# State products of a gated linear attention in three 32-column tiles per head

## The chip, the cores and the metric

The kernel runs on one core of a Trainium2 chip. The metric is the time of one execution on the device in microseconds; each figure is a median of several runs. The profile is one execution seen by the hardware profiler, with times counted from the start of its span.

## The reference

A linear attention with complex, data-dependent decay (4 sequences, 8 heads, 768 steps, head size 48) is followed by a two-layer network with an ELU between the layers, on all 3072 tokens:

```python
def _attn_ref(q, k, v, a_re, a_im):
    B, H, S, D = q.shape                          # 4, 8, 768, 48
    mag = np.sqrt(a_re * a_re + a_im * a_im)
    scale = np.minimum(mag, 0.999) / (mag + 1e-06)
    a_re_n, a_im_n = (a_re * scale, a_im * scale)
    for t in range(S):
        ar, ai = (a_re_n[:, :, t, :, None], a_im_n[:, :, t, :, None])
        new_re = ar * S_re - ai * S_im
        new_im = ar * S_im + ai * S_re
        kv = np.einsum('bhd,bhe->bhde', k[:, :, t], v[:, :, t])
        S_re, S_im = (new_re + kv, new_im)
        y[:, :, t] = np.einsum('bhd,bhde->bhe', q[:, :, t], S_re)

def _moe_ref(x, w_in, w_out):                     # x: 3072 x 384, d_ff 2048
    h = x @ w_in
    g = np.where(h > 0.0, h, np.exp(np.minimum(h, 0.0)) - 1.0)
    return g @ w_out
```

The state of a head is a complex 48 x 48 matrix. The kernel holds its real and imaginary parts one under the other, as 96 features by 48 values.

## The kernel before

The work is cut into 12 **units**, u = 0 to 11. A unit is two sequences (n = 0, 1) and 128 steps; `where(u)` gives them, and the units of a pair of sequences alternate with those of the other, so units 10 and 11 are the last 128 steps. A unit's 128 steps are two chunks (c = 0, 1) of L = 64 steps. Decays become cumulative sums of logarithms and angles (ScalarE, VectorE); keys and queries are multiplied by the decays and by cosine and sine (`gated`, L1003), which gives 96 features per head in `gates["k"]` and `gates["q"]`, one head beside the next; the key tile has 32 more columns of zeros at its end.

From these, in each unit:

- `state_products(u, n)` (L1089 to L1111): for each head and chunk, the product of keys and values over the chunk's 64 steps. The weights are 64 rows of `gates["k"]`, the streamed operand the chunk's 48 value columns of the head. The result goes to one PSUM tile `g` per chunk, 128 partitions by 8 heads by 48. In units 10 and 11 the last chunk's state isn't needed, so there is one chunk in place of two. From unit 1 on, a head and chunk take two matmuls of 64 columns each. 128 columns are read from the start of the head's 96, so the last 32 belong to the next head and their rows of the result are never used.
- the scores (in `small`, L1216; matmul at L1224): 32 matmuls of keys with queries, 96 rows, 64 columns, into the two PSUM banks that `outs` gives; `masked` (L1229) multiplies them by the causal mask.
- `state_sums` (L1113 to L1128): VectorE adds the old state to the product (L1124), GpSimd multiplies by the chunk's decay (L1126).
- values and carried state: `valued_pe` (L1237, matmul at L1145) and `carried_pe` (L1245, matmul at L1154); the latter reads the 96 feature rows of the state alone.
- `copied` and `seam` bring the result into the form in which the layers read it.

The two layers of a unit (`layer_of`, L1795) use fewer, combined products: `mult` (matmul at L1542), with sums, copies and the ELU between them (`kept` L1555, `joint` L1558, `low` L1563 and L1564, `whole_of` L1567), and `product` (L1404) with `folded` (L1382) ahead of it.

The **order** is written by hand: `plan` holds each step with a time in slots, the loop from L1837 on and `put` (L1710) fill it, `SHIFT` moves single steps, and what has the same time stays in the order in which it was put. Each engine issues its part in that order. For units 3 to 11 the stretch around the change is, on PE: `state_products(u, 0)`, the scores, `state_products(u, 1)`, then products of the layer before. In unit 4 some layer products stand between the scores and the second block; in units 10 and 11 both blocks stand ahead of the scores. The lines that place it:

```python
            put(r + 28.2, small, u)
            for n in range(NB):
                put(r + 28.2, state_sums, u, 0, (n,))
                put(r + 28.2, masked, u, n)
            put(r + 28.2, state_products, u, 1)
```

`PAIRED` is 2. Units 0 to 2 have orders of their own. The scores take the two banks of `outs`, which the layer of the unit before also uses (`opened_banks`, L1527).

Of the kernel before, what the change touches and what calls it, by code (L numbers as in the profile page):

```python
# [13 lines left out]
ALU = mybir.AluOpType  # L14
# [491 lines left out]
def kernel(  # L506
# [12 lines left out]
    nc = tc.nc  # L519
# [40 lines left out]
    F = 2 * D  # L560
# [5 lines left out]
    BL = 32  # L566
# [15 lines left out]
    def work(shape, tag="w"):  # L582
        return ps.tile(shape, FP32, tag=tag, bufs=3, name=tag)
# [4 lines left out]
    def where(u):  # L588
        return u % (B // NB) * NB, u // (B // NB) * C
# [122 lines left out]
    def new(tag, bufs=1, shape=None):  # L712
        return sb.tile(shape or [C, NB, H, D], FP32, tag=tag, bufs=bufs, name=tag)
# [306 lines left out]
    PAIRED = 2  # L1020
# [64 lines left out]
    def states(u, n):  # L1085
        state_products(u, n)
        state_sums(u, n)

    def state_products(u, n):  # L1089

        x = nat[u]
        b, s = where(u)
        x["S", n] = [state.get(b + n)]
        if s == S - C:
            last = C // L - 1
        else:
            last = C // L
        x["G", n] = gs = [
            work([C, H, D], "w" if u else "mlp")
            for c in range(last)  # L1100
        ]
        for h in range(H):
            for c, g in enumerate(gs):
                k = gates["k"][ts(c, L), ds((n * H + h) * F, C)]
                parts = [(g[ts(i, HP), h], k[:, ts(i, HP)]) for i in range(2)]
                if u == 0:
                    parts = [(g[:, h], k)]
                for to, of in parts:
                    nc.tensor.matmul(  # L1109
                        to, lhsT=of, rhs=vn[u % 2][ts(c, L), n, ts(h, D)], start=True, stop=True,  # L1110
                    )  # L1111

    def state_sums(u, n, chunks=range(C // L)):  # L1113
        x = nat[u]
        for c, g in list(enumerate(x["G", n])):
            if c not in chunks:
                continue
            old = x["S", n][-1]
            new_s = new("S", 8, [C, H, D])
            wide = x["T"][:, n, c].unsqueeze(2).to_broadcast([C, H, D])  # L1120
            if old is None:
                nc.vector.tensor_tensor(out=new_s, in0=g, in1=wide, op=ALU.mult)
            else:
                nc.vector.tensor_tensor(out=new_s, in0=g, in1=old, op=ALU.add)  # L1124
                eng = nc.vector if u < 2 else nc.gpsimd
                eng.tensor_tensor(out=new_s, in0=new_s, in1=wide, op=ALU.mult)  # L1126
            x["S", n].append(new_s)
        state[where(u)[0] + n] = x["S", n][-1]  # L1128

# [43 lines left out]
    def scored(u):  # L1173

        x = nat[u]
        t = outs()
        state_products(u, 0 if u > PAIRED else 1)
        for n in range(NB):
            for h in range(H):
                for c in range(C // L):  # L1180
                    nc.tensor.matmul(
                        t[n][ts(c, L), ts(h, L)], lhsT=keys_of(n, h, c),
                        rhs=queries_of(n, h, c), start=True, stop=True,
                    )
        if u > PAIRED:
            state_products(u, 1)
        for n in range(NB):
            state_sums(u, 0 if u > PAIRED else 1, [n])
            x["a", n] = new("a", 2, [C, H, L])
            nc.vector.tensor_tensor(  # L1190
                out=x["a", n], in0=t[n].rearrange("p (h t) -> p h t", h=H),
                in1=mask.unsqueeze(1).to_broadcast([C, H, L]), op=ALU.mult,
            )
        if u > PAIRED:
            state_sums(u, 1)
# [391 lines left out]
    def pronounced():  # L1587
# [13 lines left out]
        out=ident, in_=ident, pattern=[[-1, C]], base=0, channel_multiplier=1,  # L1601
# [20 lines left out]
    parts = [("in", m) for m in range(NF // 2)] + [("out", m) for m in range(NF // WF)]  # L1622
# [323 lines left out]
```

## Time and profile before

| what | value |
|---|---|
| time, median of 3 runs | 625.51 us (624.91 to 625.74) |
| span of the profiled execution | 622.1 us |
| PE matmuls busy | 604.0 us (97%), 6980 records |
| PE weight loads busy | 549.2 us (88%), 6980 records |
| VectorE (DVE) / ScalarE (ACT) / GpSimd (POOL) busy | 507.8 / 415.8 / 196.2 us |
| granted TensorE clock | 0.9 or more of full speed in all but one fortieth of the span |

A time is that of the whole execution, some 3.4 us above the span from the first to the last instruction that the profile shows. In the lists of instructions, a row of the timeline gives the start, the time that the merged instructions take, the engine, the line, the operation, the tiles (out<-in), the shape and the number of instructions; in brackets stands the engine's idle time before it and what ended it. "64*64" is rows by columns of the tensor engine's array that a matmul uses, "64x48" its rows by streamed columns. "issue" means that nothing that the profile shows was waited for. A row of the DMA view gives a queue's packets, their MB, and their time as a share of 16 engines over the stretch; of a stretch of 0.1 us, 100% is thus 1.6 us, and a packet counts where it starts.

### The profile page before, as it was taken

Reading aid. Unit: us, or ns where it says so; the run is one execution under the profiler, and the core shown is the slowest. Engines: PE = TensorE matmul, PEld = TensorE weight load, DVE = VectorE, ACT = ScalarE, POOL = GpSimd, SP = SyncE. Lnnn points to the kernel's source line nnn. Section 1 sums busy time; section 2 is a strip of 40 time slices with the busy share of each in tenths; the row PEclk is TensorE's granted clock in tenths of the full one; section 3 lists DMA queues with packets and bytes.
Section 4 is the critical chain, followed back from the end, with each engine's and each line's share of the span. In section 5 each row is a group of like instructions: output and inputs, shape, how many; then the busy total and the mean of one; then the engine's idle time right before and its main releaser. Section 6 shows DMA issues by size and latency. Waiting matters only on the chain. (4 is left out here: it accounts for less than half of the span.)

```text
span 622.1 us, 16987 instructions
## 1 busy us (share of the span) xinstructions
PE 604.0 (97%) x6980; PEld 549.2 (88%) x6980; DVE 507.8 (82%) x790; ACT 415.8 (67%) x681; POOL 196.2 (32%) x256
## 2 busy tenths in 40 slices
PE   8899999999999999999999999999999999999996
PEld 5778886576899999989999989998999999999996
DVE  6999999877688998988888888888788888884482
ACT  6985573776868667576777776776777777661350
POOL 2010000113123625623634534533544542522000
PEclk9899999999999999999999999999999999999999
DMA  9988669431623346355456354564574564252101
GB/s 173 181 154 144 129 174 199 111 78 44 103 42 66 62 88 141 71 121 129 96 118 140 82 120 107 117 120 97 121 122 100 136 109 116 56 95 65 54 1 32
DMA packets 192179, 65.54 MB, mean 105 GB/s; under 512 B 168116, under 2 KB 181596, under 8 KB 192092
## 3 DMA queue, kind: packets, MB, share of 16 engines
q1 hardware_dynamic: 187920, 62.72, 48.3%
q0 software_dynamic: 3520, 1.20, 1.7%
q8 instruction: 57, 0.93, 0.6%
q10 hardware_dynamic: 652, 0.44, 0.2%
q14 instruction: 30, 0.25, 0.1%
HBM read 48.91 MB, written 4.80 MB: 86 GB/s over the span
## 5 line engine op out<-in xcount | busy, mean ns | idle before, releaser
L1404 PE MATMUL mlp<-w_out,g 128*128 128x192 f32 x640 | 111.9, 328 | 0.0
L1404 PEld LDWEIGHTS mlp<-w_out,g 128*128 128x128 f32 x640 | 104.3, 190 | 3.3 <-DVE ee L1418 0.6
L1126 POOL TENSOR_TENSOR S<-S,T 128x384 f32<-128x384 f32 x36 | 38.1, 1059 | 143.3 <-DVE S L1124 84.6
L1382 DVE TENSOR_TENSOR g<-g 128x512 f32<-128x512 f32 x80 | 60.7, 774 | 6.3 <-PE mlp L1404 4.7
L1295 PE MATMUL mlp<-x,w_in 128*128 128x256 f32 x288 | 64.0, 380 | 0.2 <-DMA x<-y 0.2
L1295 PEld LDWEIGHTS mlp<-x,w_in 128*128 128x128 f32 x288 | 54.2, 190 | 8.9 <-ACT n L851 0.8
L1563 ACT ACTIVATE ee<-g 128x512 f32<-128x512 f32 x63 | 39.6, 628 | 30.1 <-DVE g L1558 27.6
L1542 PE MATMUL mlp<-x,w_in 128*128 128x128 f32 x424 | 56.6, 276 | 1.2 <-DVE o L1430 1.2
L1404 PE MATMUL mlp<-w,g 128*128 128x192 f32 x320 | 54.5, 329 | 0.0
L1275 POOL DMA_DIRECT2D x<-y x62 | 30.4, 498 | 71.6 <-ACT y L1171 39.1
L1542 PEld LDWEIGHTS mlp<-x,w_in 128*128 128x128 f32 x424 | 51.5, 192 | 1.5 <-DVE o L1430 1.4
L1404 PEld LDWEIGHTS mlp<-w,g 128*128 128x128 f32 x320 | 51.8, 190 | 0.6
L1567 DVE SCALAR_TENSOR_TENSOR g<-ee,g 128x512 f32<-128x512 f32 x63 | 44.2, 709 | 5.2 <-ACT ee L1564 5.2
L1564 ACT ACTIVATE ee<-ee 128x512 f32<-128x512 f32 x72 | 45.4, 631 | 2.3
L1555 ACT COPY g<-mlp 128x512 f32<-128x512 f32 x36 | 21.0, 586 | 25.7 <-PE mlp L1542 25.6
L1558 DVE TENSOR_TENSOR g<-g,mlp 128x512 f32<-128x512 f32 x45 | 30.4, 675 | 9.3 <-PE mlp L1542 8.1
L1542 PE MATMUL mlp<-x,g 128*128 128x128 f32 x224 | 30.0, 277 | 1.4 <-ACT g L1555 1.4
L1285 ACT ACT_TABLE_LOAD x24 | 30.8, 1283 | 0.5
L913 ACT ACTIVATE n<-w 64x384 f32<-64x384 f32 (+1 forms) x60 | 28.1, 486 | 3.8 <-PE w L898 3.0
L1262 ACT COPY x<-y 128x384 f32<-128x384 f32 x20 | 8.6, 482 | 31.4 <-PE y L1154 31.4
L1542 PEld LDWEIGHTS mlp<-x,g 128*128 128x128 f32 x224 | 27.7, 192 | 1.8 <-ACT g L1555 1.8
L1542 PE MATMUL y<-x,w_in 128*128 128x128 f32 x216 | 28.6, 275 | 0.5 <-ACT g L1555 0.5
(222 smaller groups left out, 1386.1 us busy)
## 6 DMA issues: line engine op xcount, KB each, us to landing
w<-in_moe_w_out_dram SPq DMA_DIRECT2D x8, 768.0 KB, 4.5
g<-in_moe_w_in_dram SPq DMA_DIRECT2D x24, 256.0 KB, 3.2
g<-in_moe_w_out_dram SPq DMA_DIRECT2D x24, 256.0 KB, 2.8
w<-in_moe_w_in_dram SPq DMA_DIRECT2D x16, 288.0 KB, 6.1
vn<-in_v_dram SPq DMA_DIRECT2D x24, 192.0 KB, 3.6
qt<-kt SPq DMA_DIRECT2D x72, 64.0 KB, 2.9
kt<-cs SPq DMA_DIRECT2D x72, 64.0 KB, 2.3
q<-in_q_dram SPq DMA_DIRECT2D x11, 384.0 KB, 4.5
```

Of the source, the lines that this page charges most:

```text
L913: nc.scalar.activation(out=flat(x[key][to, n : n + 1]), in_=t[of], func=AF.Exp, scale=sign)
L1126: eng.tensor_tensor(out=new_s, in0=new_s, in1=wide, op=ALU.mult)
L1275: eng.dma_start(out=x["x"][ds(j * HP + D, G), i], in_=x["y"][ds(j * HP + i * G, G)])
L1285: nc.scalar.preload_act_table_set(name)
L1295: nc.tensor.matmul(t[:, e], lhsT=w_in[:, i, ts(f + e, C)], rhs=x["x"][:, i], start=(i == 0), stop=(i == NI - 1),)
L1382: nc.vector.tensor_tensor(out=S_of(u, k, h), in0=a, in1=b, op=op)
L1404: nc.tensor.matmul(to, lhsT=a[:, m], rhs=b[:, m], start=(first and h == 0 and m == 0), stop=False, skip_group_check=True,)
L1542: nc.tensor.matmul(x["c" + c][:, ts(m, C)], lhsT=a[:, m], rhs=x["mix"][p], start=(p == BANKS[c][0] and m == 0), stop=False, skip_group_che ...
L1558: nc.vector.tensor_tensor(out=part(u, to), in0=part(u, a), in1=part(u, b), op=op)
L1563: nc.scalar.activation(out=e, in_=part(u, of), func=AF.Relu, scale=-1.0)
L1564: nc.scalar.activation(out=e, in_=e, func=AF.Exp, scale=-1.0)
L1567: nc.vector.scalar_tensor_tensor(out=part(u, to), in0=nat[u]["e", to], scalar=-1.0, in1=part(u, of), op0=ALU.add, op1=ALU.max,)
```

## The change

From the fourth unit on (u = 3 to 11), a head and chunk of `state_products` take three matmuls with 32 weight columns each, that write 32 partitions each, in place of two with 64. They cover the 96 features and nothing of the next head. `state_sums` then works on the 96 partitions that are written, in place of 128. The order of the steps stays.

```diff
@@ -1103,6 +1103,8 @@
             for c, g in enumerate(gs):
                 k = gates["k"][ts(c, L), ds((n * H + h) * F, C)]
                 parts = [(g[ts(i, HP), h], k[:, ts(i, HP)]) for i in range(2)]
+                if u > PAIRED:
+                    parts = [(g[ts(i, BL), h], k[:, ts(i, BL)]) for i in range(F // BL)]
                 if u == 0:
                     parts = [(g[:, h], k)]
                 for to, of in parts:
@@ -1118,12 +1120,16 @@
             old = x["S", n][-1]
             new_s = new("S", 8, [C, H, D])
             wide = x["T"][:, n, c].unsqueeze(2).to_broadcast([C, H, D])
+            to = new_s
+            if u > PAIRED:
+                to, g, wide = new_s[0:F], g[0:F], wide[0:F]
+                old = None if old is None else old[0:F]
             if old is None:
-                nc.vector.tensor_tensor(out=new_s, in0=g, in1=wide, op=ALU.mult)
+                nc.vector.tensor_tensor(out=to, in0=g, in1=wide, op=ALU.mult)
             else:
-                nc.vector.tensor_tensor(out=new_s, in0=g, in1=old, op=ALU.add)
+                nc.vector.tensor_tensor(out=to, in0=g, in1=old, op=ALU.add)
                 eng = nc.vector if u < 2 else nc.gpsimd
-                eng.tensor_tensor(out=new_s, in0=new_s, in1=wide, op=ALU.mult)
+                eng.tensor_tensor(out=to, in0=to, in1=wide, op=ALU.mult)
             x["S", n].append(new_s)
         state[where(u)[0] + n] = x["S", n][-1]
 
```

## Rows read from the trace of the kernel before

**Rows 1.** The page: busy time, the chain that ended last, the instruction queue (packets, MB).

```profile
PE 604.0 (97%) x6980; PEld 549.2 (88%) x6980; DVE 507.8 (82%) x790; ACT 415.8 (67%) x681; POOL 196.2 (32%) x256
...
PE mlp L1404 18%; PE mlp L1542 10%; PE y L1542 5%; PE y L1224 2%; PE y L1154 2%; PE w L1109 1%; PE y L1145 1%; PE w L846 1%; DVE g L1567 1%; DVE g L1558 1%; POOL kg L1014 1%; DMA g<-in_moe_w_in_dram 0%; DMA g<-in_moe_w_out_dram 0%; PE w L898 0%; ACT L1285 0%
```

**Rows 2.** Line L1109: xcount, then ns min/median/max of one, starts, forms.

```profile
L1109 PE MATMUL w<-vn,kg x1280: 199/218/253, 51.8 to 556.8; 64*64 64x48 f32 x183
```

**Rows 3.** Timeline of PE, the opening of unit 3.

```profile
179.34 1.15 PE L1109 MATMUL w<-vn,kg 64*64 64x48 f32 x64
180.42 2.09 PE L1224 MATMUL y<-qt,kt 96*64 96x64 f32 x64
182.43 1.15 PE L1109 MATMUL w<-vn,kg 64*64 64x48 f32 x64
183.51 0.76 PE L1404 MATMUL mlp<-w_out,g 128*128 128x192 f32 x3
```

**Rows 4.** Timeline of PE, both state blocks of unit 10.

```profile
509.34 2.07 PE L1109 MATMUL w<-vn,kg 64*64 64x48 f32 x64
```

**Rows 5.** Timeline of PE, two products with 48 weight columns (units 0 and 11).

```profile
14.80 0.88 PE L955 MATMUL w<-ident,n 128*48 128x2 f32 x16
...
565.56 1.99 PE L1154 MATMUL y<-qt,S 96*48 96x64 f32 x64
```

**Rows 6.** Timeline of PE and DVE, the opening of unit 7.

```profile
368.86 1.15 PE L1109 MATMUL w<-vn,kg 64*64 64x48 f32 x64
...
369.66 0.68 DVE L1558 TENSOR_TENSOR g<-g,mlp 128x512 f32<-128x512 f32 x1
...
370.00 2.44 PE L1224 MATMUL y<-qt,kt 96*64 96x64 f32 x64
...
372.38 0.56 PE L1109 MATMUL w<-vn,kg 64*64 64x48 f32 x24
...
373.47 0.80 PE L1109 MATMUL w<-vn,kg 64*64 64x48 f32 x40 [0.53 <-issue]
...
374.20 1.57 PE L1404 MATMUL mlp<-w_out,g 128*128 128x192 f32 x8
```

**Rows 7.** Timeline of PE, the opening of unit 8.

```profile
415.75 1.15 PE L1109 MATMUL w<-vn,kg 64*64 64x48 f32 x64
...
419.21 1.02 PE L1109 MATMUL w<-vn,kg 64*64 64x48 f32 x53
421.33 0.43 PE L1109 MATMUL w<-vn,kg 64*64 64x48 f32 x11 [1.10 <-issue]
421.69 1.57 PE L1404 MATMUL mlp<-w_out,g 128*128 128x192 f32 x8
```

**Rows 8.** Stretch between two stops: its length, then busy time (xcount) of each engine.

```profile
373.46:421.32 47.86, 46.73 (x633) 44.63 (x633) 39.35 (x64) 34.15 (x55) 22.22 (x25) 1.00 0.53 111
```

**Rows 9.** DMA queues from 180.3, 226.85, 278.3, 325.0, 370.75, 418.4, 466.3, over 0.1; then 373.46:421.32.

```profile
q8 instruction: 1, 0.02, 54.8%
...
q8 instruction: 1, 0.02, 69.2%
...
q8 instruction: 1, 0.02, 74.3%
...
q8 instruction: 1, 0.02, 70.9%
...
q1 hardware_dynamic: 106, 0.02, 99.0%
q8 instruction: 1, 0.02, 74.9%
...
q8 instruction: 1, 0.02, 83.3%
...
q8 instruction: 1, 0.02, 78.0%
...
q8 instruction: 5, 0.08, 0.8%
```

## The prediction

> **What bounds the kernel now.** I read the page first. TensorE's matmuls are busy for 97% of the span, no other engine for more than 82%, and the chain that ended last runs through PE lines, L1404 and L1542 ahead of all [rows 1]. So the kernel is bound by PE's stream: a microsecond more or less in its program order is a microsecond at the end, unless PE then meets a wait. The line of the edit has 1,280 matmul records at 64x64 [rows 2]; a float32 matmul leaves two matmul and two weight-load records, so a block of 32 matmuls (one sequence, two chunks) is 64 + 64 records.
>
> Next the PE timeline at the opening of a unit, which is where the change lies: a block of state products (S0), the scores, a second block (S1), then the layer's products [rows 3]. A block's 64 matmul records take 1.15 us, the last of them 0.22 us [rows 2, 3], so 63 steps take 0.93: 14.8 ns each, or 59 ns for the four tiles (two chunks, two column halves) that run side by side. Where the sequence has one chunk left, 64 records take 2.07 us [rows 4]: 29.4 ns each, again 59 ns per round, now of two tiles. So a tile's own turn sets the pace, and the other tiles run beside it.
>
> **What a 32-column tile costs.** No row has one. Bounds come from two neighbours. A record of 48 weight columns and 2 streamed ones comes every (0.88 - 0.18)/15 = 46 ns, so weights of 32 columns cost no more than that. A record of 48 weight columns and 64 streamed ones takes 56 ns per round of two ((1.99 - 0.22)/63 x 2), and 48 streamed columns in proportion 42 ns [rows 5]. The turn of a 64x32 tile with 48 streamed columns thus lies between 42 and 46 ns; I take 43, nearest to the streamed bound, since weights of 32 columns should load below 46. A head still needs two rounds (six tiles each, three where one chunk is left). A block of eight heads then takes 16 x 43 ns = 0.68 us in place of 0.93, provided that six tiles do run side by side; the other end is 14.8 ns per record whatever the tile, 96 x 14.8 = 1.42 us. I take 0.68, because the round's length did not change between two tiles and four.
>
> Where does this saving of 0.25 us a block land? In unit 3 on both blocks (0.5). In units 5 to 9 the scores, which begin at 370.00 in unit 7, get no further than their first matmul until DVE's L1558 frees their bank at 369.66 + 0.68 = 370.34, 1.48 us after S0 began [rows 6]. A shorter S0 only lengthens that wait, so S1 alone gains there, 0.25 each, and in unit 4 likewise. Units 10 and 11 run 32 rounds in one stretch: 32 x (59 - 43) = 0.5 each. Sum: -(0.5 + 0.25 + 5 x 0.25 + 2 x 0.5) = **-3.0 us**. DVE's and POOL's sums of states work on 96 partitions in place of 128; they have the same 384 elements in each, and I cost the difference at nothing, as PE does not wait for them here. No step, DMA or wait is moved.
>
> **What the added instructions cost.** In units 7 and 8, S1 stops in its middle, where no instruction waits for another engine: after 24 of 64 records, resuming at 373.47 [rows 6], and after 53, resuming at 421.33 [rows 7]. Between these two resumptions lie 1,266 PE records [rows 8] and five transfers of the instruction queue of 16 KB each [rows 9], so some 253 a transfer; with the dozen semaphore instructions 5 x 256 fits. Both stops, then, are the same edge of a block of 256 instructions that had not arrived. The transfer before the first stop starts at about 370.8 and takes 1.20 us (74.9% of 16 engines over 0.1 us), to 372.0; PE resumes 1.5 us later. At the second it is 418.45 + 1.33 = 419.8, and again 1.5 us later PE resumes [rows 6, 7, 9]. Counting 256 instructions back from the stops, PE had passed the edge before at 369.24 and 416.55. So passing an edge calls for the block after next, and from there to the resumption it took 4.2 and 4.8 us; PE, in dense code, got there sooner. Counting on from these edges, the same sum (start, length, 1.5 us) gives 2.8 us in unit 3 (edge 179.9), 3.5 in unit 4 (226.0), 3.3 in unit 5 (277.7), 2.9 in unit 6 (324.7) and 3.9 in unit 9 (465.2) [rows 9]. In unit 3 the data queue is idle; in unit 7 it is full beside the fetch [rows 9].
>
> Before, an opening has 3 x 128 = 384 PE instructions, and the second edge falls inside it only by luck. After, it has 192 + 128 + 192 = 512, two blocks, so **every opening of units 3 to 9 holds two edges 256 instructions apart**. Each unit also shifts the edges of the later ones by 128. Counted through the program, the first edge then lies 74, 35, 188, 118, 48, 234 and 164 instructions after S0's start in units 3 to 9. In time from S0's start, with S1 beginning at 3.5 us as in unit 7 [rows 6]: unit 5 passes its first edge at 188/192 x 0.68 = 0.67 us and reaches the second, 124 of 192 into S1, at 3.5 + 0.44 = 3.94.
>
> For the fetch I take the mean of the six loaded units, (3.5 + 3.3 + 2.9 + 4.2 + 4.8 + 3.9)/6 = 3.8 us, and 2.8 in unit 3; bounds 2.8 and 4.8. Unit 5: ready at 0.67 + 3.8 = 4.47, the 68 instructions left take 0.24, the change of tiles 0.15: 4.86, against 3.49 + 0.93 + 0.15 = 4.57 now, +0.29. Units 6 and 9 end at 4.86 too, against 4.54 now: +0.32 each. Unit 7: ready at 3.97, late in the scores, end 5.18 against 5.34 now (it loses its old stop), -0.16. Unit 8: edges at 2.10 and 4.06, ready at 5.90, end 6.13 against 5.94 now, +0.19. Unit 4: ready at 3.92 against 3.3 reached, +0.63, less 0.25: +0.38. Unit 3: ready at 3.06 against 2.88, so -0.5 shrinks to -0.31. Units 10 and 11 have one edge in their opening: -0.5 each. Sum: -0.31 + 0.38 + 0.29 + 0.32 - 0.16 + 0.19 + 0.32 - 1.0 = **+0.03 us**. The sum is against the span of 622.1 us; the median of the runs lies 3.4 above it, and I carry that over.
>
> The Trainium skill bears on this ("Runtime: NRT & Kernel Launch", section "Instruction fetch mechanics"): instructions come in 16 KiB blocks of 256, and a block's edge is said to be mostly hidden, since the next block is fetched while one executes. The block agrees with rows 9; that it is hidden does not, by the two stops.
>
> **Rivals.** *A, forecast: fetch takes back what the tiles give*, +0.03 us, 625.6. For it: the count of edges and six fetch lengths. Against: the lengths are not the new ones, as the edges are passed at other moments of the data traffic.
>
> *B, the blocks arrive in time.* New edges come earlier in the opening than the bulk of the data transfers in some units. With 2.8 us throughout: unit 3 -0.31, units 4, 5, 6 and 9 -0.25 each, unit 7 -1.0 and unit 8 -0.8 (mostly their old stops), units 10 and 11 -1.0: -4.1 us, 621.4. If blocks were always there, as the page of the skill has it, it would be -3.0 and the two stops' 2.0: -5.0 us, 620.5.
>
> *C, slower: the blocks come as late as in the two stops seen.* With their mean, 4.5 us, units 4 to 9 give +1.07, +0.99, +1.02, +0.54, +0.89, +1.02, and units 3, 10, 11 together -1.31: +4.2 us, 629.7. The place is S1 (the scores in units 4 and 7). Each 0.1 us of fetch is worth 0.6 us, so it decides from 4.0 us on. For it: these two are the only lengths that a resumption shows whole, and their edges are passed, as the new ones, within the first microsecond of an opening. Against: four other units are shorter.
>
> *D, six tiles don't overlap*, 14.8 ns per record: a block takes 1.42 us, some +1 us in each of units 3 to 9, -0.45 in units 10 and 11: about +6.1 us, 631.6. Against it: a round was 59 ns with two tiles and with four.
>
> That the change is without effect on the program is excluded: each head has three products in place of two.
>
> **How the numbers follow.** A 0.42, B 0.27, C 0.24, D 0.07. About 0.2% (1.25 us) is what a measurement of this kernel can tell from no change. A falls within it in most of its spread (0.36 of 0.42), the rest to both sides: faster 0.30, same 0.36, slower 0.34. The range leaves out the far half of B and nearly all of D: 622.0 to 629.8; A's own range, fetch 3.6 to 4.0 us, is 624.4 to 626.8.
>
> **What would show it.** Blocks of the state products of 96 records in about 0.9 us with the last one, not 1.6; in the timeline of units 4 to 9 a stop marked "issue" inside S1, or late in the scores in units 4 and 7, 1.5 us after an instruction transfer ends; units 10 and 11 half a microsecond shorter. Stops over 1 us in most units are C, none is B. The prediction is wrong in its steps if the stops sit elsewhere, or if the openings keep their length and the time moves in the layer's products.

## The result and the profile after

The kernel with the change takes 633.04 us (median of four runs, 631.25 to 634.07), against 625.3 us for the kernel before, measured beside it: a ratio of fast runs of 1.0131, 95% interval 1.011 to 1.0152 (the two medians alone give 1.012). It is slower by 7.7 us, outside the range of the prediction. The nearest number is that of rival D (631.6), but the profile below doesn't bear out D's mechanism; it shows that of C, with a larger loss. The profiled execution has a span of 632.3 us and a time of 634.06, which is 1.0 above the median.

Lines of the file move by six behind the change: the products of states are at L1111, the scores at L1230, the sums at L1130 (VectorE) and L1132 (GpSimd). First the page of the kernel after: busy time, TensorE's granted clock in 40 slices, and the instruction queue (packets, MB, share).

```profile
PE 606.2 (96%) x7492; PEld 549.7 (87%) x7492; DVE 505.9 (80%) x790; ACT 415.8 (66%) x681; POOL 207.2 (33%) x256
...
PEclk9899999999999999999999999998999999999999
...
q8 instruction: 61, 1.00, 0.7%
```

PE has 512 records more than in [rows 1]: 32 for each of the 14 blocks of units 3 to 9, and 32 for each of units 10 and 11. Its busy time grew by 2.2 us, while the span grew by 10.2. What was added is time in which PE stood still. The waits of PE by line (total us, times, longest us) name it:

```profile
PE w L1111 <- issue: 7.0, 4, 2.3
PE y L1230 <- issue: 2.4, 5, 1.7
```

"Issue" means that no semaphore was waited for. Before, only the two stops of [rows 6, 7] stood on the products' line, 1.6 us together. PE's timeline shows where the new ones lie. Units 4 (one row), 5, 6, 7, 8, 9 and 10 of the kernel after (start us, us, engine, line, operation, tiles, records, idle before):

```profile
228.49 0.68 PE L1230 MATMUL y<-qt,kt 96*64 96x64 f32 x14 [0.26 <-issue]
...
276.89 1.09 PE L1111 MATMUL w<-vn,kg 64*32 64x48 f32 x96
278.13 2.39 PE L1230 MATMUL y<-qt,kt 96*64 96x64 f32 x64 [0.15 <-issue]
280.44 0.79 PE L1111 MATMUL w<-vn,kg 64*32 64x48 f32 x62
283.13 0.47 PE L1111 MATMUL w<-vn,kg 64*32 64x48 f32 x34 [1.90 <-issue]
283.53 0.76 PE L1410 MATMUL mlp<-w_out,g 128*128 128x192 f32 x3
...
328.64 0.44 PE L1111 MATMUL w<-vn,kg 64*32 64x48 f32 x27
329.92 0.84 PE L1111 MATMUL w<-vn,kg 64*32 64x48 f32 x69 [0.84 <-issue]
...
373.47 1.09 PE L1111 MATMUL w<-vn,kg 64*32 64x48 f32 x96
374.76 2.15 PE L1230 MATMUL y<-qt,kt 96*64 96x64 f32 x56 [0.21 <-DMA g<-in_moe_w_in_dram]
378.63 0.45 PE L1230 MATMUL y<-qt,kt 96*64 96x64 f32 x8 [1.72 <-issue]
379.01 1.09 PE L1111 MATMUL w<-vn,kg 64*32 64x48 f32 x96
...
425.14 0.99 PE L1111 MATMUL w<-vn,kg 64*32 64x48 f32 x85
428.43 0.30 PE L1111 MATMUL w<-vn,kg 64*32 64x48 f32 x11 [2.30 <-issue]
...
471.90 1.09 PE L1111 MATMUL w<-vn,kg 64*32 64x48 f32 x96
473.14 2.39 PE L1230 MATMUL y<-qt,kt 96*64 96x64 f32 x64
475.46 0.69 PE L1111 MATMUL w<-vn,kg 64*32 64x48 f32 x50
478.12 0.64 PE L1111 MATMUL w<-vn,kg 64*32 64x48 f32 x46 [1.97 <-issue]
...
520.24 1.56 PE L1111 MATMUL w<-vn,kg 64*32 64x48 f32 x96
521.82 2.39 PE L1230 MATMUL y<-qt,kt 96*64 96x64 f32 x64
```

Every unit from 5 to 9 stops, and each stop sits on the predicted instruction. In unit 5 it was to be 124 of 192 instructions into the second block (S1). A matmul record comes with one weight load, so that is after 62 of 96 records, and the row says x62. Counted likewise, S1 should stop after 27, 85 and 50 records in units 6, 8 and 9, and the rows say x27, x85 and x50. In unit 7 the stop is late in the scores, after 56 of 64 records, also as counted. Units 3 and 4 stop as well, for less: in unit 4 the scores stop after 50 records, where 14 are left as in the first row, and in unit 3 a step of 0.31 us between two records stands after the fifth record of S1. Both are the counted places (291 and 330 instructions after the start of S0). A block of 96 records takes 1.09 us with its last one, so D, which had 1.6, is out. So the edges of the blocks of 256 instructions are real, and what went wrong is how long a block takes to come.

That length is the time from passing the first edge of an opening (in S0; in unit 8 in the scores, 2.2 us after the start of S0) to the resumption at the second. In unit 5 the edge is at 277.77 (188 of 192 instructions into S0) and PE resumes at 283.13: 5.36 us. Units 6 to 9 give 4.29, 4.97, 4.66 and 5.45, the mean of the five 4.95. The prediction took 3.8. Unit 4, with 3.7 us, is close to that, and unit 3 took 3.1. The queues at the moment the block's transfer starts, in the openings of units 5 and 9 (packets, MB, share of 16 engines over 0.1 us, so 100% is 1.6 us):

```profile
q8 instruction: 1, 0.02, 82.4%
q1 hardware_dynamic: 28, 0.00, 33.6%
...
q1 hardware_dynamic: 106, 0.02, 117.1%
q8 instruction: 1, 0.02, 60.8%
```

In unit 5 the transfer begins at about 280.45 and takes 82.4% of 1.6 us, 1.32 us; PE resumes 1.4 us after its end, close to the 1.5 of [rows 6, 7, 9] (1.3 to 1.6 in the five units). Between the edge and the start of the transfer, though, lie 2.7 us. In the five units this delay is 2.68, 1.73, 2.25, 1.72 and 2.93 us: the long part of a fetch, and the one that varies, is the time until its transfer starts.

The time from the start of S0 to the next products of the layer (in unit 4, to the end of S1) moved thus:

| unit | 3 | 4 | 5 | 6 | 7 | 8 | 9 | 10 | 11 | sum |
|---|---|---|---|---|---|---|---|---|---|---|
| predicted, us | -0.31 | +0.38 | +0.29 | +0.32 | -0.16 | +0.19 | +0.32 | -0.50 | -0.50 | +0.03 |
| measured, us | +0.22 | +0.45 | +2.07 | +1.06 | +1.22 | +1.13 | +2.25 | -0.20 | -0.18 | +8.02 |

In units 10 and 11 the state blocks alone are shorter by 0.42 and 0.43 us, but the scores behind them then take 2.3 us in place of 2.1 to the start of the next products. Unit 10, PE before and after, and VectorE after:

```profile
511.34 2.16 PE L1224 MATMUL y<-qt,kt 96*64 96x64 f32 x64
513.43 1.57 PE L1404 MATMUL mlp<-w_out,g 128*128 128x192 f32 x8
```

```profile
524.13 1.57 PE L1410 MATMUL mlp<-w_out,g 128*128 128x192 f32 x8
```

```profile
521.26 0.68 DVE L1564 TENSOR_TENSOR g<-g,mlp 128x512 f32<-128x512 f32 x1
```

The scores now begin at 521.82, before VectorE's L1564 ends at 521.94, and a step of 0.26 us stands behind their first matmul. This fits the wait for the bank that the prediction read from [rows 6]; it reckoned with it in units 5 to 9 and not here.

The openings hold 8.0 us of the 10.2 by which the two profiled executions differ. The medians differ by 7.7, since the execution shown after lies 1.0 above its median, and the one shown before probably lies below its own: in all kernels profiled later the time is 1.8 us above the span, so a span of 622.1 would be a time of 623.9, not the 625.5 that I carried over. Another part of the 10.2 is a clock that the kernel before did not show at this place. Behind the stop of unit 8 PE runs for some microseconds at the lower of its two levels (stretch: length, busy time of PE, weight loads, DVE, ACT and POOL with their counts, granted clock, DMA share, GB/s):

```profile
428.50:440.00 11.50, 11.50 (x166) 10.61 (x167) 11.03 (x16) 5.43 (x9) 6.32 (x4) 0.85 0.59 126
```

A mean of 0.85 between 1.2 and 2.4 GHz is 11.5 x 0.15 / 0.5 = 3.5 us at the lower, worth 1.7 us. Unit 8 as a whole grew by 2.8 us, its opening by 1.13; the difference is this. PE had stood 2.3 us just before, the longest stop of the profile. About half a microsecond of the 10.2 was not located.

### The profile page after: what moved, and what is told of

It reads as the page before. It is cut to its first block, busy times and chain, and to the rows that moved or that the text cites. A ratio compares the mean times of both kernels' runs of the same rounds, so it can differ in the third digit from the quotient of the medians.

```text
span 632.3 us, 18011 instructions
## 1 busy us (share of the span) xinstructions
PE 606.2 (96%) x7492; PEld 549.7 (87%) x7492; DVE 505.9 (80%) x790; ACT 415.8 (66%) x681; POOL 207.2 (33%) x256
## 5 line engine op out<-in xcount | busy, mean ns | idle before, releaser
L1132 POOL TENSOR_TENSOR S<-S,T 96x384 f32<-96x384 f32 (+1 forms) x36 | 50.2, 1395 | 143.0 <-DVE S L1130 85.3
L1388 DVE TENSOR_TENSOR g<-g 128x512 f32<-128x512 f32 x80 | 57.2, 729 | 6.3 <-PE mlp L1410 4.7
L1564 DVE TENSOR_TENSOR g<-g,mlp 128x512 f32<-128x512 f32 x45 | 30.4, 676 | 9.4 <-PE mlp L1548 8.1
L1130 DVE TENSOR_TENSOR S<-w,S 96x384 f32<-96x384 f32 (+1 forms) x38 | 20.8, 549 | 13.2 <-PE w L1111 12.0
L1111 PE MATMUL w<-vn,kg 64*32 64x48 f32 (+1 forms) x1792 | 24.3, 210 | 7.2 <-issue 7.0
L1111 PEld LDWEIGHTS w<-vn,kg 64*32 64x32 f32 (+1 forms) x1792 | 20.9, 109 | 11.3 <-issue 10.3
```

What stands on the lines that cost most here:

```text
L1111: nc.tensor.matmul(to, lhsT=of, rhs=vn[u % 2][ts(c, L), n, ts(h, D)], start=True, stop=True,)
L1132: eng.tensor_tensor(out=to, in0=to, in1=wide, op=ALU.mult)
L1388: nc.vector.tensor_tensor(out=S_of(u, k, h), in0=a, in1=b, op=op)
L1564: nc.vector.tensor_tensor(out=part(u, to), in0=part(u, a), in1=part(u, b), op=op)
```

## The experiments

### Two tiles that cover 96 features: 64 and 32 columns

```diff
-    parts = [(g[ts(i, BL), h], k[:, ts(i, BL)]) for i in range(F // BL)]
+    parts = [(g[0:HP, h], k[:, 0:HP]), (g[HP:F, h], k[:, HP:F])]
```

> The changed kernel with a head's 96 features in two products, of 64 and of 32 columns, in place of three of 32: as many PE instructions as before, but the state sums on 96 partitions, as changed. Theory (the loss is waiting for instruction blocks, called for by 128 more instructions per opening): the stops of 1.0 to 2.5 us in the second state block go, and the time is that of before, 625.3 us within 1 us. Rival (the 96-partition state sums, whose GpSimd operations take 1.4 us in place of 1.06, or a 32-column tile as such, make the loss): 631 to 633 us, as with the change.

Measured: 781.31 us, ratio 1.249 [1.2455, 1.2524]. Neither theory has this. The instructions are as many as before and the columns as many as after; what is new is that a 64-column and a 32-column tile alternate. PE's timeline in unit 5 of this kernel:

```profile
317.79 8.71 PE L1111 MATMUL w<-vn,kg 64*64 64x48 f32 x64
```

A block of 64 records takes 8.7 us, where it took 1.15 in [rows 3]. The granted clock is 0.73 in this stretch, which at most doubles a time; it does not make 1.15 into 8.7. While the clock was still at 1.00, in the first 3.8 us of this block, 35 records started, 0.11 us each. The block changes its tile's width 32 times, so by an estimate a change costs some (8.71 - 1.15) / 32 = 0.24 us in the mean of this stretch. The Trainium skill ("TensorEngine Tiling (Array Packing)", section "Key Properties") says that a change of the tiling mode, not of the tile alone, drains TensorE; the row fits that, and gives a change a size, though it does not show the drain itself. As a test of the fetch this run says nothing, so its two questions were put again: the number of instructions by "one wide product" below, the 96 partitions by a run of their own.

### The second block later by a slot

```diff
-            put(r + 28.2, state_products, u, 1)
+            late = 29.2 if 4 < u < NU - 2 else 28.2
+            put(r + late, state_products, u, 1)
...
-                put(r + 28.2, state_sums, u, 1, (n,))
+                put(r + late, state_sums, u, 1, (n,))
```

This stands on the kernel after. It keeps every instruction and puts some of the layer's products, which take longer per instruction, between the scores and S1.

> The changed kernel with the second state block of units 5 to 9 moved behind two of the layer's products (8 matmuls, 2.6 us). Theory: in units 5, 6, 8 and 9 the second block edge is reached 2.6 us later, so their stops of 2.1, 1.0, 2.5 and 2.2 us vanish, and unit 7, whose edge lies in the scores, keeps about 2 us: 625 to 627 us. Rival (tile rate or state sums): 631 to 633 us, since nothing of these is changed; or slower still, if the later state sums hold up the carried products.

Measured: 628.49 us, 1.0058 [1.0038, 1.0077], 4.5 us less than the change. No stop is left on the products' line; on the scores' line 2.6 us remain, 2.1 of them those of units 4 and 7 (0.63 and 1.51), ahead of which nothing was moved. So the cost sits in S1 because dense code gets there before the block does. The time did not come down as far as expected; one cost of a later S1 shows in the combinations below.

### The load of the values later

The data queue that is full beside the fetch carries, among others, the load of the next values (`load_v`), which the kernel issues in the twelfth slot of a unit. Here it is issued 2.5 slots later; nothing else differs from the kernel after.

```diff
-        put(r + (8 if u < PAIRED + 3 else 12), load_v, u)
+        put(r + (8 if u < PAIRED + 3 else 14.5), load_v, u)
```

> The changed kernel with the load of the next unit's values (two transfers of 192-byte pieces) issued 2.5 slots later, behind the opening in place of ahead of it, from unit 5 on. Theory: with the data queues emptier at the block edges, a block arrives 2.8 to 3.5 us after its edge in place of 4.3 to 5.5, and of the stops of units 5 to 9 (2.0, 1.0, 2.0, 2.5, 2.2 us) about 1.5 us each goes: 625 to 628 us. Rival (a block takes as long whatever the data transfers do): 631 to 633 us.

Measured: 626.53 us, 1.0021 [1.0003, 1.0038]: 6.5 us less than the change, by moving one transfer. The stretch of 3.5 us from the start of S0 in unit 5, first in the kernel after, then in this one (columns as above; DMA share and GB/s are last):

```profile
276.90:280.40 3.50, 3.31 (x161) 3.07 (x160) 3.23 (x6) 2.74 (x6) 0.82 (x1) 1.00 0.94 203
```

```profile
275.40:278.90 3.50, 3.31 (x161) 3.03 (x160) 3.19 (x7) 2.74 (x6) 0.83 (x1) 1.00 0.26 78
```

PE and the other engines do the same in both, with the DMA engines busy for 0.94 of the time in the one and 0.26 in the other. The fetches now take 4.35, 3.5, 2.8 and 4.2 us in units 5, 6, 8 and 9 (in unit 7, where the timeline marks no stop, the first record of the new block starts 3.3 us after the edge): a mean of 3.6 instead of 4.95. The stops shrink with them. In unit 9, where PE stood 1.97 us on the same instruction:

```profile
466.99 0.69 PE L1111 MATMUL w<-vn,kg 64*32 64x48 f32 x50
468.28 0.64 PE L1111 MATMUL w<-vn,kg 64*32 64x48 f32 x46 [0.60 <-issue]
```

So the value load makes the fetch longer, by some 1.3 us in the mean, and moving it takes away most of the loss. It is not the whole cause. In unit 5 of this run the block's transfer starts 1.6 us after the edge, although the DMA engines were as good as empty for the last 1.2 us of that (DMA share and GB/s last):

```profile
276.60:277.80 1.20, 1.16 (x32) 1.05 (x34) 1.20 (x3) 1.17 (x3) 0.00 (x0) 1.00 0.00 0
```

What else holds a transfer back stays open. And in unit 9 of the kernel after, the fetch took 5.45 us from an edge that was passed at 472.67; the loads of queries and keys had been issued just before, that of the values came 2.1 us after (SP issues the transfers):

```profile
470.99 0.62 SPq L612 DMA_DIRECT2D q<-in_q_dram  x1
471.65 1.52 SPq L612 DMA_DIRECT2D k<-in_k_dram  x1
...
474.76 2.40 SPq L608 DMA_DIRECT2D vn<-in_v_dram  x2
```

With the value load moved, unit 9 still took 4.2 us. Other bulk loads may thus lengthen a fetch too; no run moved them.

### Three tiles in units 10 and 11 alone

`u > 9` in place of `u > PAIRED`, at both places of the change.

> Three 32-column products in units 10 and 11 alone, where one chunk is left (three tiles side by side in place of two, a round of 43 ns in place of 59); units 3 to 9 as before. Theory: -0.5 us in each of the two units and no new stop, as their opening holds one block edge: 624.3 us. Rival (32-column tiles cost more as such): 625.3 us or more.

Measured: 624.1 us, 0.9989 [0.997, 1.0007]. The interval reaches 1. In the profile both units have the rounds of 43 ns, and the two stops of the kernel before are still there. The expected 624.3 us came out by luck: the kernel before, measured again beside it, was at 624.62 and not at 625.3, so by medians the gain is 0.5 us, not the microsecond of the expectation and not clear of noise. The rounds are as fast as reckoned; the wait for the bank takes back half of what they give, as in the kernel after.

### Sums on 96 partitions alone

The kernel before, with its two 64-column products, and the second half of the change (`to`, `g`, `wide` and `old` cut to 96 partitions).

> The kernel before, with the state sums on 96 partitions from unit 3 on, as changed, and the products in two 64-column tiles, as before. Theory (the loss is in the instruction blocks): GpSimd's part takes 1.4 us in place of 1.06 for each, but nothing waits for it: the time of before, 624.6 us within 1 us, and stops in units 7 and 8 alone. Rival (the sums make the loss or a part of it): 626 us or more.

Measured: 624.34 us, 0.9994 [0.9981, 1.0007]. The sums cost nothing that can be told from noise, in line with the prediction. Beside the stops of units 7 and 8 there is one of 0.3 us ahead of unit 3. GpSimd's multiplication by the decay has a higher mean in the kernel after, 1,395 ns against 1,059, and the same shows here. Its distribution (ns min/median/max of one, first and last start, forms) shows that most of these operations are not slower:

```profile
L1130 POOL TENSOR_TENSOR S<-S,T x36: 825/828/2944, 139.5 to 561.8; 96x384 f32<-96x384 f32 x32, 128x384 f32<-128x384 f32 x4
```

The median is 828 ns, before 831; a few last up to 2.9 us, before up to 1.5. What they share GpSimd or memory with was not looked into, since nothing on the critical chain waits for them.

### One product of 96 columns per head

On the kernel after, for units 3 to 9: one wide tile, so half the instructions of the kernel before, and fewer tiles that could run side by side.

```diff
                 if u > PAIRED:
+                    parts = [(g[0:F, h], k[:, 0:F])]
+                if u > 9:
                     parts = [(g[ts(i, BL), h], k[:, ts(i, BL)]) for i in range(F // BL)]
```

> The changed kernel with one product of 96 columns per head and chunk in units 3 to 9, in place of three of 32: 64 PE instructions a block in place of 192, so an opening has 256 and one block edge. A tile of 96 weight columns should take some 85 ns a turn (46 for 48 columns, 59 for 64), two side by side, 1.37 us a block in place of 0.89 with the change. Theory: no stop at a block edge in any opening; against the kernel before +0.9 us in unit 3, +0.4 to 0.5 in each of units 4 to 9, -2.0 for the two old stops, -0.9 in units 10 and 11: 625 to 626 us, although each block takes half a microsecond longer than with the change (633 us). Rival (the stops are a wait for something else in the second state block, or the loss is in the tiles' pace): stops of 1 to 2.5 us stay, or the time is above 633 us, since the blocks are longer.

Measured: 625.18 us, 1.0008 [0.9994, 1.0021]. PE's timeline at the opening of unit 5:

```profile
277.67 1.56 PE L1113 MATMUL w<-vn,kg 64*96 64x48 f32 x32
279.16 2.08 PE L1232 MATMUL y<-qt,kt 96*64 96x64 f32 x64
281.17 1.56 PE L1113 MATMUL w<-vn,kg 64*96 64x48 f32 x32
282.66 0.76 PE L1412 MATMUL mlp<-w_out,g 128*128 128x192 f32 x3
```

A block takes 0.4 us longer than with two tiles (42.5 ns a record, of which only the two chunks run side by side), and no opening of the units 5 to 9 has a stop. An opening has 256 instructions here, so a second edge falls into none. The scores of this unit take 2.08 us in place of 2.39: behind the longer S0 the step after their first matmul is gone. That S1 with the slowest products stops nowhere, and with the most instructions stops in units 3, 5, 6, 8 and 9, tells the supply of instructions from the cost of tiles.

### Combinations, from the kernel before on

Four more kernels use what the runs showed: three tiles only in units 10 and 11, with the value load at 14.5; the same with S1 of units 5 to 9 a slot later; the kernel before with the load at 14.5 alone; and the first of these with one 96-column product in S0 of units 5 to 9.

> Three 32-column products in units 10 and 11 alone (as in the run before, 624.1 us), and the load of the next unit's values issued behind the opening. Theory: with two 64-column tiles in units 3 to 9 the edges lie as before; the stops of units 7 and 8 (0.7 to 1.3 us in a run) shrink as the blocks come 1 to 1.5 us sooner: 622 to 623 us. Rival (the load's place matters only by chance): 624.1 us.

Measured: 621.82 us (621.37 to 624.62), 0.9962 [0.9944, 0.9979]. It beats both kernels. The old stops in units 7 and 8 are gone from the waits on the products' line; the one row of 0.3 us that is left there lies at 139.44, ahead of unit 3. S1 of unit 8 is one row now, but 0.4 us longer than the 1.15 of a block without a stop, so a short stop is left inside it, and one of 0.3 us in unit 7:

```profile
420.04 1.53 PE L1111 MATMUL w<-vn,kg 64*64 64x48 f32 x64
```

> As the run before, and the second state block of units 5 to 9 behind two of the layer's products. Theory: what is left of the stops goes, if any is: 622 to 623 us, at most 0.5 below the run before. Rival (later state sums hold up the carried products, or VectorE's order suffers): 624 us or more.

Measured: 625.77 us, 1.0019 [1.0003, 1.0036], 4 us worse than without the spacing: S1 a slot later has a price of its own. One row of it is to be seen in the waits of PE, in unit 9, which the kernel without the spacing does not have:

```profile
PE w L898 <- DVE S L1130: 1.2, 1, 1.2
```

With S1 the sums of states come later, and PE's next use of their buffers waits for them. The spaced kernel above has the same wait, 1.0 us, which is a part of why it stayed over its expected time. The other 2.8 us were not located.

> The kernel before with nothing but the load of the next unit's values issued 2.5 slots later. Theory: its two stops (0.7 and 1.3 us in the profile) shrink to 0.3 to 0.4 us each and nothing else moves: 1 to 2 us below the kernel before, and some 1 us above the version that also has the 32-column products in units 10 and 11. Rival (the gain of that version came from elsewhere): no difference to before.

Measured: 622.85 us, 0.9972 [0.9954, 0.999]. The kernel before loses its stop in unit 7 and all but 0.1 us of that in unit 8. So the value load delayed its instructions too, and moving it alone is worth about 2 us (0.6 to 2.9 by the interval), about what the two stops took.

> The best version so far (load later, 32-column products in units 10 and 11) with the first state block of units 5 to 9 in one 96-column product per head and chunk: 64 PE instructions in place of 128, 1.37 us in place of 0.93, which the scores' wait for VectorE's L1558 should hide. Theory: edges shift, units 5, 7 and 9 hold one edge in their opening and units 6 and 8 two that are 3.2 to 3.4 us apart, so the stops left are 0.3 us or less: 621 to 622 us, 0 to 0.6 below the version without it. Rival (the longer first block costs its 0.44 us in each of five units): 624 us.

Measured: 622.79 us, 0.9966 [0.9954, 0.9978]. S0 takes 0.4 us longer, S1 starts 3.50 us after S0 as before, and no opening stops. The longer S0 is hidden by the scores' wait for their bank, as the prediction argued from [rows 6], and there is no gain over the kernel without it.

## Why the prediction was wrong

**The edges: right.** Blocks of 256 instructions, two edges in each opening, and the place of every stop in units 3 to 9 were counted from two stops of the profile before, to the record. This was the mechanism of the loss, and the runs confirm it from three sides: longer products with fewer instructions have no stop, the same instructions spread out have none in S1, and a data queue with less in it shortens them.

**The length of a fetch: the step that failed.** "For the fetch I take the mean of the six loaded units ... 3.8 us". Measured: 4.29 to 5.45, mean 4.95, above even the upper bound of 4.8 in three units. The difference to 3.8, 1.56 + 0.49 + 1.17 + 0.86 + 1.65, is 5.7 of the 8.0 us by which the openings came out above the forecast. The six lengths were those of edges that lay anywhere in an opening. Of the five new ones, four lie in the first microsecond of theirs, when a bulk load has just been issued (that of the values in units 5 to 7, that of queries and keys in unit 9); in unit 8 the edge comes 2.2 us after the start of S0, and the value load 0.5 us after it. The prediction says much of this itself, as an argument for C ("their edges are passed, as the new ones, within the first microsecond of an opening"), and as one against A; of unit 8 its own reckoning, edges at 2.10 and 4.06, has it otherwise. The two fetches that met this condition had taken 4.2 and 4.8 us, and they were the sample to use; the mean mixed them with fetches under other conditions. The bound, too, should have reached beyond the largest of two values. C had the right mechanism and the right condition (it decides from 4.0 us on), but not the size: its 629.7 was still 3.3 us short.

**The pace of six tiles: failed in part.** "Provided that six tiles do run side by side", a block was to take 0.68 us, 43 ns a round. With three tiles (units 10 and 11) the round is (1.56 - 0.20) / 32 = 42.5 ns, as predicted (the last record takes 0.20 us), and the blocks of these units gain 0.42 and 0.43 of the 0.50. With six, 96 records take 1.09 - 0.20 = 0.89 us, 56 ns a round. From start to start of its records, the second to the fourth round of a block take 42 to 43 ns; after the first 32 records the spacing is 10 ns a record on average (63 steps in 0.63 us), which is 60 a round. The six tiles do run side by side, and then something else sets the pace, perhaps the rate at which PE is given instructions once a first stock of them is used up; that was not tested. With it S1 gains 0.04 in place of 0.25 us a unit, and unit 3, which also has its stop of 0.31 us, loses its gain. Units 5 to 9 take another 0.1 to 0.3 us each as well, since S0 is slower to reach the edge and what is left of S1 is slower behind it: 1.0 us together, of the 2.3 that the fetch lengths leave.

**Units 10 and 11: the overlap was wrong.** They were put at -0.5 us each, with no wait behind them, and came out at -0.20 and -0.18. By the rows above the shorter blocks bring the scores to their bank before VectorE has freed it, which takes back 0.23 and 0.26 us; the rest is the rounds. Together the two units are 0.6 us short of the forecast.

**No cost from the sums on 96 partitions: right**, by a run of its own.

**The clock: not foreseen.** It fell behind one long stop and cost some 1.7 us in the profiled execution. Whether it falls in every execution is not shown.

The Trainium skill's rule ("Runtime: NRT & Kernel Launch", section "Instruction fetch mechanics") that a block's edge is mostly hidden is not borne out in dense code: the two rows of waits shown above hold 7.0 + 2.4 us of this kernel's 632, 9.0 of them at edges. For the kernel as a whole the word fits: of 61 instruction transfers on the page, seven belong to the stops in the openings of units 3 to 9.

## What to carry to other kernels

Short TensorE instructions are not free even when they run side by side: count the instructions between two edges of 256 against the time that they take. In this kernel a fetch took 4.3 to 5.5 us beside a bulk load, and 2.8 to 4.4 us with one such load moved away; where 256 instructions run in less than that, expect a stop. Look also at what stands behind a product that gets shorter: in units 10 and 11 half of the gain went into a wait for a bank. A large load issued just ahead of such a stretch delayed the instructions themselves here; moving that load can be worth more than the tiling, as it was here (0.3% on the kernel before, without touching a product). And a mean over samples is a poor estimate when the case at hand shares its conditions with two of them only: take those two.

## What was unexpected of the hardware

- Products that alternate between 64- and 32-column tiles took 121 to 166 ns a record, in part at the lower clock, where a single width takes 14.8.
- Of a fetch of 5 us, the transfer itself is 1.0 to 1.4 us and the step from its end to the first instruction 1.3 to 1.6; what grows is the time before it starts, 1.7 to 2.9 us under load.
- 64x32 tiles ran at 43 ns a round in threes. In sixes they did so for some 30 records only, and at 60 ns on average from there on.
- Behind a stop of 2.3 us PE ran for about 3.5 us at the lower clock, in a stretch where the kernel before ran at the full one. It lost some 1.7 us by it.
